# Six sets of products of ones in the early steps, four weight pieces' low halves on TensorE, maxima subtracted on VectorE, and a new order of all steps

## Chip, cores and metric

One core of a Trainium2 chip runs the whole kernel. The metric is device microseconds of one execution, median of several runs.

## What is computed

Attention over four sequences of 768 positions with 8 heads of 64, where each query sees its neighbours nearer than 16 positions and 24 block summaries (maximum of 32 keys, mean of 32 values), followed by a two-layer MLP with gelu on the 3072 tokens:

```python
k_sum = k.reshape(B, H, nb, block, D).max(axis=3)
v_sum = v.reshape(B, H, nb, block, D).mean(axis=3)
mask_l = np.abs(pos[:, None] - pos[None, :]) < window
scores_s = scale * np.einsum('bhsd,bhnd->bhsn', q, k_sum) + np.log(block)
a = np.exp(scores_all - np.max(scores_all, axis=-1, keepdims=True))
a = a / (np.sum(a, axis=-1, keepdims=True) + 1e-09)
x = np.matmul(a, v_all)                       # to tokens x 512
h = x @ w_in                                  # 512 x 2048
g = 0.5 * h * (1.0 + erf(h / sqrt(2)))
return g @ w_out                              # 2048 x 512
```

w_in and w_out come as 64-bit floats, q, k and v as 32-bit ones.

## The kernel before, in words

The attention is cut into 24 units: unit u is 256 queries of 4 heads, two units make the 256 tokens of a chunk, so chunk c needs units 2c and 2c+1. The first six units compute in f32 on TensorE (steps `f_mask`, `f_scores`, `f_sums`, `f_values`), the others with f16 high and low halves. A unit goes: `f_mask` writes the band's mask into the PSUM tile `pss` (there is one such tile for all units), `f_scores` adds 16 small products, `evac` (ScalarE) copies the scores to SBUF, `maximum` (GpSimd, PARTITION_ALL_REDUCE) takes the maximum over the keys, then the maximum is subtracted and the exponential taken; `f_sums` and `f_values` write the PSUM tile `psv` (one for all units); `norm_take`, `norm_cross`, `norm_rec`, `norm_spread`, `norm_mult` divide by the sums; `x_hi` (ScalarE) and `x_lo` (VectorE) split the result.

In the kernel before the maximum of units 0 to 3 is subtracted on TensorE (`m_shift`, a product of a row of -1 with the maximum, into `pss`) and the exponential reads PSUM (`m_exponent`); from unit 4 on VectorE subtracts (`shift`) and `exponent` reads SBUF. Units 6 and 7 too get their mask by `f_mask` and `evac`.

A piece i of w_in (256 of 2048 columns) goes: `fetch_w_in` (1 MiB), three VectorE steps `wi_bits` that make f32 of the 64-bit words, `wi_hi` (ScalarE, high half to f16), `wi_lo` (VectorE, the rest to f16). `wo_bits`, `wo_hi`, `wo_lo` do the same with w_out. `phase1 c i` is 24 products of chunk c with piece i (high by high, high by low, low by high), `gelu`, `g_hi`, `g_lo` follow, and `phase2` is the second layer. Chunks 4 to 11 get their first layer by a Strassen scheme (`sp`), with sums of weights from `wt_add`, `wt_hi`, `wt_lo`.

Keys' maxima come from `prep_k` (VectorE, from the transfer `fetch_k`), `prep_k_end` splits them (a CAST and a subtraction), `k_pack` (ScalarE) builds the f32 keys of a unit, `sum_vt` (TensorE) sums the values of the first sequence's blocks.

The order of all steps is a string of some 1,670 names, ORDER, which is issued as it stands; each engine and the one DMA queue (SyncE's) works its own steps off in that order, and semaphores let a step wait for its inputs and for the room of its output. Three lines of the program that a reader needs:

```python
self.k32 = kp0[:, r0 : r0 + NR, s0 : s0 + CH + TQ].rearrange(...)   # keys of units 0 to 3: the first fetch_k
ps_h = ctx.enter_context(tc.tile_pool(name="ps_h", bufs=N_PSH, space=PSUM))   # three tiles "psh", in turn
nc.gpsimd.partition_all_reduce(out_ap=self.m32, in_ap=self.s32, channels=P, reduce_op=bass_isa.ReduceOp.max)
```

`setup` opens with 16 products of ones (64x512) on TensorE, into a `psh` tile that nothing reads.

Of the kernel before, what the change touches and what calls it, by code (L numbers as in the profile page):

```python
# [77 lines left out]
sum_vt 0, wi_bits 5 0, wt_add 3 1, wt_add 3 2, wi_lo 3, load_v 0, wi_hi 2, wt_hi 3, evac 1, maximum 1, fetch_vt 2,
wi_bits 5 1, wt_lo 3, load_q 2, sum_vt 1, norm_take 0, norm_cross 0, k_pack 2, m_shift 1, m_exponent 1, sum_vt 2,
norm_rec 0, norm_spread 0, wi_bits 6 0, wi_bits 5 2, wi_bits 6 1, wi_lo 2, wi_hi 5, mean_vt, s_load_vs 0, wi_bits 6 2,  # L80
fetch_w_in 4 4, wi_lo 5, f_mask 2, f_scores 2, evac 2, wi_bits 4 0, wi_bits 4 1, maximum 2, load_v 1, s_load_vs 1,
f_values 0, norm_mult 0, x_hi 0, fetch_w_in 0 0, k_pack 3, f_sums 1, norm_take 1, x_lo 0, load_v 2, norm_cross 1,
wi_bits 4 2, m_shift 2, load_q 3, f_values 1, wi_bits 0 0, m_exponent 2, norm_rec 1, norm_spread 1, f_mask 3,
norm_mult 1, wi_bits 0 1, wi_hi 4, f_scores 3, fetch_w_in 1 1, x_hi 1, x_lo 1, wi_bits 0 2, wi_bits 1 0, evac 3,
fetch_v 1 1, f_sums 2, phase1 0 3, wi_hi 0, wi_hi 6, norm_take 2, fetch_w_in 7 3, wi_bits 1 1, load_k 4, wi_lo 6,
load_vs 2, prep_v 1 1, f_values 2, fetch_k 1 3, norm_cross 2, phase1 0 2, k_sums 0 0, norm_rec 2, norm_spread 2,
phase1 0 5, load_v 3, wi_bits 1 2, fetch_k 1 1, gelu 0 3, norm_mult 2, maximum 3, m_shift 3, wi_hi 1, load_v 4,
m_exponent 3, wi_lo 0, prep_k 1 3, phase1 0 6, gelu 0 5, wi_lo 1, wi_bits 7 0, load_vs 3, prep_k 1 1, f_sums 3,
norm_take 3, wi_bits 7 1, fetch_k 1 2, x_hi 2, f_values 3, load_q 4, prep_k 1 2, gelu 0 2, g_hi 0 3, fetch_v 1 2, g_lo
0 3, g_hi 0 2, norm_cross 3, norm_rec 3, g_hi 0 5, phase1 0 0, x_lo 2, k_pack 4, fetch_k 1 0, norm_spread 3, norm_mult  # L90
3, x_hi 3, phase1 0 1, gelu 0 1, fetch_v 1 0, wi_bits 7 2, g_lo 0 5, g_hi 0 1, x_lo 3, load_vs 4, f_mask 4, f_scores
4, wi_hi 7, evac 4, gelu 0 6, prep_k 1 0, maximum 4, wi_lo 7, phase1 1 3, prep_v 1 2, f_mask 5, prep_v 1 0, g_lo 0 2,
g_hi 0 6, gelu 1 3, g_lo 0 1, g_lo 0 6, load_k 5, fetch_w_out 1 5, wo_bits 1 0, k_pack 5, shift 4, fetch_w_out 0 4,
load_k 6, phase1 1 7, g_hi 1 3, wo_bits 1 1, phase1 0 7, gelu 1 7, g_hi 1 7, g_lo 1 7, exponent 4, wo_bits 1 2, gelu 0
7, wo_bits 0 0, wo_bits 0 1, wo_bits 0 2, load_q 5, phase1 1 1, gelu 0 0, g_hi 0 0, f_sums 4, g_hi 0 7, f_values 4,
gelu 1 1, wo_hi 1, g_lo 0 0, norm_take 4, f_scores 5, norm_cross 4, g_lo 0 7, phase1 1 6, g_hi 1 1, evac 5, wo_lo 1,
gelu 1 6, s_k_hi 6, fetch_w_out 3 5, wi_lo 4, norm_rec 4, load_q 7, load_v 6, phase1 1 2, norm_spread 4, norm_mult 4,
fetch_w_out 2 4, g_lo 1 3, phase1 1 4, maximum 5, wo_hi 0, wo_lo 0, f_mask 6, gelu 1 2, phase1 1 5, load_mask, k_lo 6,
fetch_v 1 3, shift 5, load_v 5, exponent 5, prep_k_end 1 0, load_k 8, wo_bits 3 0, g_lo 1 1, wo_bits 3 1, phase1 1 0,
gelu 1 0, g_hi 1 2, prep_v 1 3, wo_bits 3 2, phase2 0 0, g_hi 1 6, k_sums 1 0, load_vs 5, gelu 1 5, g_hi 1 5, f_sums  # L100
5, wo_hi 3, wo_bits 2 0, g_lo 1 2, norm_take 5, wo_bits 2 1, phase1 0 4, s_q_hi 7, x_hi 4, wo_bits 2 2, wo_hi 2, wo_lo
3, load_vs 6, q_lo 7, scores 6, s_k_hi 8, wo_lo 2, prep_k_end 1 1, fetch_w_out 5 5, f_values 5, k_sums 0 1, k_lo 8,
x_lo 4, phase2 0 1, norm_cross 5, evac 6, maximum 6, norm_rec 5, norm_spread 5, norm_mult 5, fetch_w_out 4 4, phase2 0
3, gelu 1 4, wo_bits 5 0, v_hi 6, wo_bits 5 1, f_mask 7, x_hi 5, x_lo 5, g_hi 1 4, g_lo 1 4, gelu 0 4, g_lo 1 5,
phase2 0 2, phase1 2 4, wo_bits 4 0, g_lo 1 6, gelu 2 4, phase1 2 1, wo_bits 4 1, wo_bits 4 2, load_v 8, load_k 7,
s_k_hi 7, phase1 2 0, g_hi 0 4, wo_hi 4, gelu 2 1, load_q 8, wo_bits 5 2, wo_hi 5, shift 6, wo_lo 4, load_vs 8, phase1
2 2, fetch_w_out 7 5, g_hi 1 0, g_lo 0 4, wo_lo 5, s_q_hi 8, gelu 2 0, g_lo 1 0, phase2 0 4, exponent 6, s_p_hi 6,
k_lo 7, phase1 2 6, v_lo 6, fetch_w_out 6 4, k_sums 1 1, scores 7, q_lo 8, v_hi 8, p_lo 6, gelu 2 6, sums 6, wo_bits 7
0, wo_bits 6 0, wo_bits 7 1, load_k 9, wo_bits 6 1, wo_bits 6 2, values 6, s_k_hi 9, evac 7, phase2 0 5, phase1 2 7,
wo_bits 7 2, wo_hi 6, wo_lo 6, wo_hi 7, fetch_k 2 3, load_q 9, g_hi 2 0, load_v 7, load_vs 7, wo_lo 7, k_lo 9, scores  # L110
8, norm_take 6, add_mask 8, phase2 0 6, norm_cross 6, norm_rec 6, norm_spread 6, s_q_hi 9, g_hi 2 1, phase2 0 7, store
0 0, maximum 7, v_lo 8, q_lo 9, shift 7, exponent 7, s_p_hi 7, phase2 1 0, norm_mult 6, load_q 11, s_q_hi 11, phase2 1
2, g_hi 2 4, phase2 1 4, wt_add 4 0, put 0 0, prep_k 2 3, p_lo 7, sums 7, v_hi 7, store 0 1, fetch_v 2 0, v_lo 7,
wt_add 4 1, wt_add 4 2, load_v 9, put 0 1, load_k 11, load_vs 9, g_lo 2 4, g_hi 2 6, norm_take 7, g_lo 2 1, g_lo 2 0,
prep_v 2 0, maximum 8, x_hi 6, phase2 1 6, gelu 2 2, phase1 2 5, norm_cross 7, norm_rec 7, x_lo 6, store 1 0, shift 8,
scores 9, gelu 2 7, q_lo 11, exponent 8, values 7, fetch_v 2 2, wt_hi 4, phase2 1 1, norm_spread 7, wt_lo 4, phase2 1
3, phase2 1 5, add_mask 9, prep_v 2 2, norm_mult 7, load_q 10, phase2 1 7, load_v 11, g_hi 2 2, s_q_hi 10, s_p_hi 8,
s_k_hi 11, load_vs 11, p_lo 8, sums 8, values 8, v_hi 9, v_lo 9, maximum 9, shift 9, fetch_k 2 1, k_lo 11, prep_k 2 1,
g_hi 2 7, g_lo 2 7, scores 11, exponent 9, put 1 0, x_hi 7, phase1 2 3, norm_take 8, load_k 10, x_lo 7, phase1 3 7,
g_lo 2 6, q_lo 10, gelu 2 5, load_v 10, add_mask 11, norm_cross 8, norm_rec 8, fetch_k 2 2, s_p_hi 9, norm_spread 8,  # L120
p_lo 9, s_k_hi 10, phase1 3 5, gelu 2 3, norm_mult 8, store 1 1, gelu 3 5, prep_k 2 2, prep_k_end 2 1, sums 9,
norm_take 9, x_hi 8, phase2 2 1, k_lo 10, scores 10, fetch_k 2 0, put 1 1, values 9, maximum 11, g_hi 2 3, g_lo 2 3,
g_hi 2 5, norm_cross 9, shift 11, exponent 11, wt_add 5 0, s_p_hi 11, load_vs 10, load_k 12, norm_rec 9, norm_spread
9, phase1 3 4, load_q 12, s_q_hi 12, g_lo 2 5, gelu 3 7, v_hi 10, phase1 3 0, gelu 3 4, v_hi 11, g_hi 3 4, norm_mult
9, g_lo 2 2, phase2 2 3, x_hi 9, wt_add 1 0, phase1 3 3, wt_add 1 1, wt_add 1 2, p_lo 11, g_hi 3 5, q_lo 12, wt_hi 1,
add_mask 10, sums 11, gelu 3 3, v_lo 11, g_hi 3 3, prep_k 2 0, phase2 2 5, load_v 12, g_lo 3 4, fetch_v 2 1, phase1 3
6, norm_take 11, wt_add 5 1, norm_cross 11, g_lo 3 3, k_sums 2 1, prep_k_end 2 0, k_sums 2 0, load_q 13, gelu 3 0,
# [111 lines left out]
def band_summary_attention_gelu_mlp(  # L239
# [85 lines left out]
    def setup():
        nc.gpsimd.memset(ones, 1.0)
        if N_FILL:

            fill = ps_h.tile([P, DM], F32, tag="psh", name="psh_fill")
            for _ in range(N_FILL):  # L330
                nc.tensor.matmul(
# [965 lines left out]
```

## Time and profile before

| | us |
|---|---|
| median of 3 runs | 587.44 (587.12 to 587.65) |
| the profiled execution | 588.54 |
| its span, first to last instruction | 586.8 |
| TensorE busy (mean granted clock 0.974) | 568.8 |
| VectorE busy | 459.2 |
| ScalarE busy | 386.5 |
| GpSimd busy | 87.5 |

The span is 1.74 us under the profiled execution's own time, and that time 1.10 us over the median. TensorE is busy 97% of the span; the page's 40 slices show it below 90% in the first three and the last only, and its granted clock below full in the first four. VectorE is busy 8 or 9 tenths up to the middle of the span.

### The profile page before, as it was taken

To read this page: it belongs to the slowest core of one execution; us is meant where nothing else is said; L and a number is where in the kernel's file an instruction comes from. 1 tells how busy PE (TensorE), PEld (TensorE's weight loads), DVE (VectorE), ACT (ScalarE), POOL (GpSimd) and SP (SyncE) were. 2 spreads that over 40 slices of the span, in tenths; PEclk is the share of its full clock that TensorE was granted. 3 is DMA by queue.
4 is the path that set the end of the run, shared out by engine and by line. 5 is a ranking of instruction groups with operands and counts; after the bars stand their busy time and mean duration, and the time that the engine had idled before them with its cause. 6 is when DMAs were issued, how large, how long until landed. Compare 5 with 4: busy or idle time off the path is not lost.

```text
span 586.8 us, 13450 instructions
## 1 busy us (share of the span) xinstructions
PE 568.8 (97%) x5784; PEld 392.8 (67%) x5784; DVE 459.2 (78%) x621; ACT 386.5 (66%) x648; POOL 87.5 (15%) x42
## 2 busy tenths in 40 slices
...
GB/s 290 328 245 279 165 209 292 194 168 131 147 146 167 82 42 159 100 116 121 75 85 75 85 133 4 56 99 79 74 62 1 20 19 19 1 18 2 2 1 91
DMA packets 28652, 64.27 MB, mean 110 GB/s; under 512 B 2736, under 2 KB 7600, under 8 KB 28592
## 3 DMA queue, kind: packets, MB, share of 16 engines
...
## 4 chain that ended last, share of the span: by engine, by line
PE 92%; ACT 2%; POOL 2%; DMA 2%; DVE 2%; issue 1%; POOLq 0%; DVEq 0%; ACTq 0%
PE psy L939 13%; PE pso L987 12%; PE pso L989 11%; PE pso L988 11%; PE psz L939 7%; PE psh L868 5%; PE psh L869 5%; PE psh L870 5%; PE pso_y L1152 4%; PE psx L939 3%; PE pss L649 3%; PE psv L793 3%; PE pss L716 2%; PE pss_x L1152 2%; POOL m L740 2%; DMA q<-in_qd_dram 2%
## 5 line engine op out<-in xcount | busy, mean ns | idle before, releaser
L740 POOL PARTITION_ALL_REDUCE m<-s x24 | 81.3, 3386 | 331.9 <-DVE s L731 113.0
L987 PE MATMUL pso<-w_out_h,gg 128*128 128x512 f16 x320 | 121.5, 380 | 0.0
L988 PE MATMUL pso<-w_out_l,gg 128*128 128x512 f16 x320 | 121.3, 379 | 0.0
L989 PE MATMUL pso<-w_out_h,gg 128*128 128x512 f16 x320 | 121.3, 379 | 0.0
L939 PEld LDWEIGHTS <-wt 128*128 128x128 f16 x768 | 74.5, 98 | 13.6 <-issue 0.8
L868 PE MATMUL psh<-xos,ww 128*128 128x256 f16 x256 | 70.9, 277 | 0.0
L869 PE MATMUL psh<-xos,ww 128*128 128x256 f16 x256 | 70.8, 277 | 0.0
L870 PE MATMUL psh<-xos,ww 128*128 128x256 f16 x256 | 70.8, 276 | 0.0
L939 PE MATMUL psy<-xos,wt 128*128 128x256 f16 x576 | 69.3, 273 | 0.0
L939 PEld LDWEIGHTS <-ww 128*128 128x128 f16 x576 | 55.1, 98 | 11.8 <-issue 0.6
L989 PEld LDWEIGHTS <-gg 128*128 128x128 f16 x320 | 31.3, 98 | 37.8
L987 PEld LDWEIGHTS <-gg 128*128 128x128 f16 x320 | 31.3, 98 | 33.7 <-issue 1.5
L988 PEld LDWEIGHTS <-gg 128*128 128x128 f16 x320 | 31.3, 98 | 31.6
L950 ACT ACTIVATE ww<-psy 128x512 f32<-128x512 f32 x48 | 28.1, 590 | 31.1 <-PE psy L939 30.8
L971 DVE SCALAR_TENSOR_TENSOR gg<-g,gg 128x512 f16<-128x512 f32 x48 | 34.8, 731 | 13.4 <-ACT gg L967 13.4
L957 DVE TENSOR_TENSOR g<-psz,ww 128x512 f32<-128x512 f32 x24 | 16.4, 685 | 20.3 <-PE psz L939 17.6
L967 ACT ACTIVATE gg<-g 128x512 f16<-128x512 f32 x48 | 29.3, 623 | 3.2 <-PE pso L988 2.6
L877 ACT ACTIVATE g<-psh 128x512 f32<-128x512 f32 x32 | 18.8, 594 | 16.8 <-PE psh L870 14.5
L868 PEld LDWEIGHTS <-ww 128*128 128x128 f16 x256 | 25.4, 99 | 6.2 <-issue 2.0
L964 ACT ACTIVATE g<-g 128x512 f32<-128x512 f32 x36 | 22.2, 622 | 8.8 <-DVE g L957 8.8
L869 PEld LDWEIGHTS <-ww 128*128 128x128 f16 x256 | 25.4, 99 | 3.8
L870 PEld LDWEIGHTS <-ww 128*128 128x128 f16 x256 | 25.4, 99 | 3.3
...
## 6 DMA issues: line engine op xcount, KB each, us to landing
...
```

Source lines behind the costliest of these rows:

```text
L740: nc.gpsimd.partition_all_reduce(out_ap=self.m32, in_ap=self.s32, channels=P, reduce_op=bass_isa.ReduceOp.max)
L868: nc.tensor.matmul(ph[:, e, :], wh, xh, start=(k == 0), stop=False)
L869: nc.tensor.matmul(ph[:, e, :], wh, xl, start=False, stop=False)
L870: nc.tensor.matmul(ph[:, e, :], wl, xh, start=False, stop=(k == NCC - 1))
L939: nc.tensor.matmul(ps[:, e, :], ws, xx, start=(first and e == 0 and k == 0 and m == 0), stop=(k == 1 and m == 2), skip_group_check=True,)
L950: nc.scalar.activation(snaps[b, q, n], split8(acc[b, q, "y"]), AF.Copy)
L967: nc.scalar.activation(g_part(o // 2, q, 0, slice(o % 2, 4, 2)), g32t[b, q, o], AF.Copy, scale=SC_G)
L971: nc.vector.scalar_tensor_tensor(out=g_part(o // 2, q, 1, fs), in0=g32t.pop((b, q, o)), scalar=SC_G, in1=g_part(o // 2, q, 0, fs), op0=ALU ...
L987: nc.tensor.matmul(p, gh, w_out_h[:, f, :], start=(f == 0), stop=False)
L988: nc.tensor.matmul(p, gh, w_out_l[:, f, :], start=False, stop=False)
L989: nc.tensor.matmul(p, gl, w_out_h[:, f, :], start=False, stop=(f == NFC - 1))
L1152: nc.tensor.matmul(ps[:, j, :], g, ww_, start=(first and e == 0 and k == 0), stop=(e == 1 and k == 2), skip_group_check=True,)
```

## The change

Three switches turn, a helper for products of ones is made out of `setup`'s loop, and ORDER is another string from its first step to its last:

```diff
-PE_DIFF = 0
-PE_SHIFT = 1
-M16_ROOM = 0
+PE_DIFF = 1
+PE_SHIFT = 0
+M16_ROOM = 1
...
 N_FILL = 16
+N_FILL_STEP = 6
...
-load_q 6, s_q_hi 6, q_lo 6, load_m16, fetch_k 0 0, prep_k 0 0, fetch_w_in 3 3, f_mask 0, load_q 0, prep_k_end 0 0,
-k_pack 0, f_scores 0, fetch_w_in 2 2, wi_bits 3 0, wi_bits 3 1, fetch_k 0 1, wi_bits 3 2, fetch_w_in 5 5, load_q 1,
...
+fetch_k 0 0, prep_k 0 0, k_pack 0, fill 3, prep_k_end 0 0, k_sums 0 0, load_q 0, fill 4, load_m16, fetch_w_in 2 2,
...
+    def products_of_ones(name, n):
+        t = ps_h.tile([P, DM], F32, tag="psh", name=f"psh_fill_{name}")
+        for _ in range(n):
+            nc.tensor.matmul(
+                t[:D].rearrange("p (n d) -> p n d", d=D), ones, ones.unsqueeze(1).broadcast_to([P, DM // D, D]),
+                start=True, stop=True,
+            )
+
+    def fill(k):
+        products_of_ones(k, N_FILL_STEP)
```

Of the steps, these differ in number: `m_shift` and `m_exponent` of units 0 to 3 go, `shift` and `exponent` of these units come (VectorE and ScalarE); `f_mask` and `evac` of units 6 and 7 go, `add_mask` of these units comes (VectorE adds the mask while it reads PSUM); `wi_lo` of pieces 0 to 3 goes, and for each half of these pieces `wi_diff` and `wi_dlo` come; `load_eye` (64 KB), `load_neg` and the six `fill` steps come. Two functions that stood unused before:

```python
def wi_diff(i, h):     # TensorE: 128 * piece - high half, into a psh tile
    nc.tensor.matmul(flat, eye, wt[:, i, h * 512 : (h + 1) * 512], start=True, stop=False)   # f32, 128x512
    nc.tensor.matmul(flat, neg, w_part(i, 0, ks), start=False, stop=True)                    # f16, 128x512
def wi_dlo(i, h):      # ScalarE: to f16
    nc.scalar.activation(w_part(i, 1, ks), flat.rearrange("p (k n) -> p k n", k=2), AF.Copy)
```

With M16_ROOM the small mask lies in the room of `w_out_l`, whose first piece is written after `f_mask 5`.

**TensorE from the scores of unit 0 to the sums of unit 0** (`pss` scores, `kf` keys, `psv` sums and values, `psw` is wi_diff's tile, `eye` and `neg` its constants, `psh_vt` the blocks' sums of v). Before:

```order
L649 MATMUL pss_0_133<-q32_0_138,kf_0_143 128x64 x16
L697 MATMUL pss_0_133<-m32_0_179,neg_1_77 128x512 x2
L620 LDWEIGHTS mask16_sb_78
L620 MATMUL pss_1_192<-mask16_sb_78 128x2x64
...
L649 MATMUL pss_1_192<-q32_1_168,kf_1_188 128x64 x16
L671 MATMUL psv_0_215<-s32_0_177,ones_f_82 32x256 x4
L532 MATMUL psh_vt_220<-w_out_h_87,w_out_l_88 88x512 x4
```

The same place in the change:

```order
L657 MATMUL pss_0_151<-q32_0_139,kf_0_124 128x64 x16
L628 LDWEIGHTS w_out_l_88
L628 MATMUL pss_1_183<-w_out_l_88 128x2x64
...
L426 MATMUL psw_2_0_189<-wt_84,eye_77 128x512
L427 MATMUL psw_2_0_189<-ww_83,neg_78 128x512
L426 MATMUL psw_2_1_212<-wt_84,eye_77 128x512
...
L331 MATMUL psh_fill_5_217<-ones_79 64x512
L331 MATMUL psh_fill_2_226<-ones_79 64x512
L657 MATMUL pss_1_183<-q32_1_192,kf_1_209 128x64 x16
L679 MATMUL psv_0_255<-s32_0_180,ones_f_82 32x256 x4
```

Between the mask of unit 1 and its scores there now stand both halves of piece 2's difference and twelve products of ones (each set is six rows as the one shown); the subtraction of the maximum is gone from TensorE.

**ScalarE at the same place** (L407 and L415 are wi_hi, L727 and L735 evac, L633/L635 and L641/L643 k_pack, L703 m_exponent, L756 exponent, L432 wi_dlo, L526 k_sums, L357 load_neg). Before:

```order
L633 ACTIVATE kf_0_143<-w_out_l_88 128x10x64
L635 ACTIVATE kf_0_143<-ks_f_81 128x2x4x32
L407 ACTIVATE ww_83<-wt_84 128x4x256
L727 ACTIVATE s32_0_177<-pss_0_133 128x1024
L633 ACTIVATE kf_1_188<-w_out_l_88 128x10x64
L635 ACTIVATE kf_1_188<-ks_f_81 128x2x4x32
L703 ACTIVATE s32_0_177<-pss_0_133 128x1024
```

Now:

```order
L641 ACTIVATE kf_0_124<-w_out_l_88 128x10x64
L643 ACTIVATE kf_0_124<-ks_f_81 128x2x4x32
L526 ACTIVATE k_hi0_90<-ks16_0_0_134 128x2x4x24
L526 ACTIVATE k_lo0_92<-ks16_0_0_134 128x2x4x24
L415 ACTIVATE ww_83<-wt_84 128x4x256
L735 ACTIVATE s32_0_180<-pss_0_151 128x1024
L357 ACTIVATE neg_78<-eye_77 128x128
L432 ACTIVATE ww_83<-psw_2_0_189 128x2x256
L641 ACTIVATE kf_1_209<-w_out_l_88 128x10x64
L643 ACTIVATE kf_1_209<-ks_f_81 128x2x4x32
L756 ACTIVATE s32_0_180<-s32_0_180 128x1024
L735 ACTIVATE s32_1_253<-pss_1_183 128x1024
```

In both, the high half of the first piece stands ahead of the copy of unit 0's scores.

**VectorE in the change, from the subtraction of unit 0's maximum to that of unit 1's** (L753 is shift, L380/L385/L389 the three steps of wi_bits, L822 norm_take, L513 prep_k, L521/L522 prep_k_end, L418 wi_lo, L838 norm_rec):

```order
L753 TENSOR_TENSOR s32_0_180<-s32_0_180,m32_0_215 128x1024
L385 SCALAR_TENSOR_TENSOR wt_84<-x32s_85,wt_84 128x1024
L389 SCALAR_TENSOR_TENSOR wt_84<-gg_89,wt_84 128x1024
L389 SCALAR_TENSOR_TENSOR wt_84<-x32s_85,wt_84 128x1024
L822 STREAM_TRANSPOSE dent_0_262<-psv_0_255 128x256
L513 TENSOR_REDUCE ks32_1_194<-kp_1_0_200 128x24
L521 CAST ks16_1_0_265<-ks32_1_194 128x48
L522 TENSOR_TENSOR ks16_1_0_265<-ks32_1_194,ks16_1_0_265 128x48
L418 SCALAR_TENSOR_TENSOR ww_83<-wt_84,ww_83 128x4x256
L838 RECIPROCAL rc_0_275<-rc_0_275 128x16
L753 TENSOR_TENSOR s32_1_253<-s32_1_253,m32_1_295 128x1024
```

The two subtractions are new on VectorE, and the transpose of unit 0's sums (L822) now has a piece of the second sequence's keys behind it.

**The DMA queue's first transfers** are, before: q of unit 6 (256 KB), the small mask (80 KB), the keys of heads 0 to 3 (784 KB), w_in piece 3 (1024 KB), q of unit 0 (256 KB), w_in piece 2; in the change: the keys of heads 0 to 3, q of unit 0, the small mask, w_in piece 2, `eye` (64 KB), a piece of the second sequence's keys (392 KB), w_in piece 0, the keys of heads 4 to 7 (784 KB), w_in piece 5. From ORDER: the first chunk's `phase1` goes 3, 2, 5, 6, 0, 1 before, then `phase1 1 3`, then `f_mask 5`; in the change 0, 5, 4, 2, 1, 7, 3, then `f_mask 5`, then `phase1 1 2`. Before, `norm_take` of a unit stands ahead of its `f_values`; in the change `f_values 2` stands ahead of `norm_take 2`, which therefore waits for it (one tile, `psv`).

## Rows read from the trace of the kernel before

**Rows 1.** Busy time by stretch of the early part: stretch, length, then busy us (and instructions) of PE, PEld, DVE, ACT, POOL, the granted TensorE clock, DMA share, GB/s.
```profile
12.00:23.00 11.00, 5.25 (x35) 3.60 (x34) 10.79 (x13) 4.31 (x6) 3.35 (x1) 0.50 0.94 342
23.00:28.50 5.50, 5.50 (x44) 4.01 (x43) 2.96 (x3) 2.67 (x3) 0.00 (x0) 0.50 0.93 359
28.50:32.00 3.50, 3.50 (x8) 1.18 (x5) 2.09 (x4) 2.27 (x8) 3.22 (x1) 0.50 0.70 179
32.00:37.00 5.00, 5.00 (x15) 1.58 (x13) 5.00 (x5) 1.85 (x2) 0.00 (x0) 0.98 1.04 404
37.00:46.00 9.00, 6.21 (x110) 4.45 (x109) 7.44 (x12) 7.40 (x14) 4.76 (x2) 0.99 0.53 187
46.00:51.60 5.60, 5.56 (x42) 3.80 (x42) 4.15 (x5) 2.47 (x3) 0.00 (x0) 0.50 0.86 285
51.60:56.00 4.40, 4.40 (x25) 3.15 (x22) 3.90 (x5) 4.29 (x11) 0.00 (x0) 0.50 0.91 342
```

**Rows 2.** The timeline of PE: start us, us, engine, line, operation, in square brackets the idle time before and what ended it. L649 f_scores, L620 f_mask, L697 m_shift, L671 f_sums, L663 f_values, L532 sum_vt, L868 the first of phase1's three lines (24 products from 63.98 on are one phase1, the next starts at 66.77 with another step).
```profile
0.94 5.56 PE L331 MATMUL psh_fill<-ones 128*64 128x512 f16 x16 [0.94 <-POOL warm L335]
6.43 0.61 PE L620 MATMUL pss<-mask_sb 128*128 128x128 f16 x4
11.55 3.58 PE L649 MATMUL pss<-q,kf 64*128 64x64 f32 x32 [4.51 <-DMA q<-in_qd_dram]
19.70 2.07 PE L697 MATMUL pss<-m,neg 1*128 1x512 f32 x4 [4.57 <-POOL m L740]
34.97 1.95 PE L532 MATMUL psh_vt<-w_out_h,w_out_l 128*88 128x512 f32 x4
37.28 2.00 PE L649 MATMUL pss<-q,kf 64*128 64x64 f32 x32
43.73 1.13 PE L697 MATMUL pss<-m,neg 1*128 1x512 f32 x4 [1.93 <-POOL m L740]
44.79 1.15 PE L663 MATMUL psv<-s,v 128*64 128x64 f32 x32
63.98 0.28 PE L868 MATMUL psh<-xos,ww 128*128 128x256 f16 x1
66.70 0.64 PE L671 MATMUL psv<-s,ones_f 128*32 128x256 f32 x8
74.29 0.60 PE L620 MATMUL pss<-mask_sb 128*128 128x384 f16 x4
76.75 0.28 PE L868 MATMUL psh<-xos,ww 128*128 128x256 f16 x1
```

**Rows 3.** The products of ones by line, 0 to 4 us and 4.6 to 6.5 us: line, engine, operation, shapes, count, then busy us, mean ns.
```profile
L331 PE MATMUL psh_fill<-ones 128*64 128x512 f16 x8 | 3.6, 634 | 0.9 <-POOL warm L335 0.9
L331 PE MATMUL psh_fill<-ones 128*64 128x512 f16 x8 | 2.1, 417 | 0.0
```

**Rows 4.** The timeline of DVE.
```profile
8.05 1.75 DVE L505 TENSOR_REDUCE ks_f<-w_out_l 128x48 f32<-128x1536 f32 x1 [3.21 <-DMA w_out_l<-in_kp_dram]
10.76 0.69 DVE L372 TENSOR_SCALAR wt<-gg 128x1024 int32<-128x1024 int32 x1 [0.50 <-DMA gg<-in_w_in_dram]
11.49 1.23 DVE L377 SCALAR_TENSOR_TENSOR wt<-gg,wt 128x1024 int32<-128x1024 int32 x1
18.26 1.43 DVE L513 CAST ks<-ks_f 128x48 f16<-128x48 f32 x1
75.33 0.68 DVE L848 TENSOR_TENSOR xos<-x32s,xos 128x512 f16<-128x512 f32 x1
75.94 0.94 DVE L505 TENSOR_REDUCE ks<-kp 128x24 f32<-128x768 f32 x1
76.80 1.21 DVE L410 SCALAR_TENSOR_TENSOR ww<-wt,ww 128x1024 f16<-128x1024 f32 x1
```

**Rows 5.** The timelines of ACT and POOL.
```profile
14.01 1.06 ACT L407 ACTIVATE ww<-wt 128x1024 f16<-128x1024 f32 x1 [3.69 <-DVE wt L381]
15.17 1.03 ACT L727 ACTIVATE s<-pss 128x1024 f32<-128x1024 f32 x1
...
16.29 3.35 POOL L740 PARTITION_ALL_REDUCE m<-s  x1 [14.31 <-ACT s L727]
```

**Rows 6.** Groups by line over the whole span: busy us, mean ns of one. L745 shift, L814, L830, L834 the norm steps, L841 the fourth of them (norm_mult), L513 prep_k_end's cast in the later sequences, L554 prep_v, L886 g_lo, L748 the loads of a table before an exponential.
```profile
L745 DVE TENSOR_TENSOR s<-s,m 128x1024 f32<-128x1024 f32 x20 | 24.3, 1217 | 1.8 <-POOL m L740 1.8
L814 DVE STREAM_TRANSPOSE dent<-psv 128x256 f32<-128x256 f32 x24 | 10.7, 447 | 21.1 <-PE psv L807 9.2 <-PE psv L671 7.8 <-PE psv L793 4.0
L834 DVE STREAM_TRANSPOSE dent<-rc 128x512 f32<-128x512 f32 x24 | 17.0, 708 | 0.6
L830 DVE RECIPROCAL rc<-rc 128x16 f32<-128x16 f32 x24 | 5.9, 245 | 2.8 <-ACT rc L827 2.7
L554 DVE TENSOR_REDUCE vs<-vb 96x32 f32<-96x1024 f32 x12 | 14.4, 1208 | 0.6 <-DMA vb<-in_vb_dram 0.6
L513 DVE CAST ks<-ks 128x48 f16<-128x48 f32 x6 | 1.5, 249 | 0.0
L841 DVE TENSOR_TENSOR x32s<-psv,dent 128x512 f32<-128x512 f32 x24 | 16.5, 686 | 2.7 <-PE psv L793 1.5 <-PE psv L663 0.6
L886 DVE SCALAR_TENSOR_TENSOR gg<-g,gg 128x512 f16<-128x512 f32 x32 | 21.9, 696 | 0.5 <-ACT gg L880 0.4
L748 ACT ACT_TABLE_LOAD x18 | 23.1, 1283 | 0.3
```

More of the change, by code (lines that the diff above doesn't have):

```diff
@@ L78 @@
[L78 to L127, printed above, removed]
```

277 lines of the change are left out of this document (162 added, 115 removed).

## The prediction

> **What bounds the kernel now.** I read the busy times by engine first: TensorE is busy 568.8 of 586.8 us, so time can be won only where it idles or where its clock is half. The slices put both into the first 57 us. The windows of that stretch [rows 1] show where: the granted clock is 0.50 (1.2 of 2.4 GHz) from 12 to 32 us and 0.50 again from 46 to 56, and about 0.98 between. The timeline of TensorE [rows 2] names the holes: 4.51 us ahead of the scores of unit 0 (a transfer of q), 4.57 us ahead of the first subtraction of a maximum (GpSimd's maximum), 1.93 us ahead of the second one, and smaller ones. After phase1 1 3 starts at 76.75 TensorE doesn't idle again before the end of the span, so what follows takes 586.8 - 76.75 = 510.05 us, and the change, which leaves the steps behind this point nearly as they are in kind and number, must be judged by when the same point is reached. VectorE is the second engine to watch: it is busy 10.79 of 11 us from 12 to 23 and 5.00 of 5 from 32 to 37 [rows 1].
>
> **The work that is added and removed.** On TensorE at full clock: two records are one f32 product. The one most like wi_diff's is sum_vt's, whose records take 1.95/4 = .49 us; a subtraction's, with one row, follow each other by .27 (four between 43.73 and 44.79) [rows 2]. I take .43, near the first, so a wi_diff is .86 + .21 for its f16 product (as one of ones, below): 1.07, between .75 and 1.19. Eight of them are 8.6 us. A product of ones took .45 us at half clock and .27 at the later rate [rows 3], between .21 (half of .45 less the change) and .27: a set of six is 1.3 to 1.6 us, six sets 7.7 at 1.28. Gone are four subtractions of 1.13 [rows 2], 4.4, and the masks of units 6 and 7, 2 x .6. TensorE gets about 10.7 us **more** work, nearly all before 50 us. It counts only where TensorE comes last.
>
> VectorE gets four subtractions of 1.22 [rows 6] and loses four wi_lo of 1.21 [rows 4]; even. ScalarE gets eight wi_dlo of 512 elements, between half and all of the 1.03 that a copy of 1024 out of PSUM takes [rows 5] (I take .6, near the half), and four table loads of 1.28 [rows 6], in a stretch where it is idle half the time [rows 1]: nothing.
>
> **When the early stage ends.** I follow the new order by hand, each step starting when its engine and its inputs are there.
>
> *To 16 us.* The keys come first in the queue. Before, DVE took them at 8.05 [rows 4] with 336 KB ahead, which is .8 to 1.1 us at the 300 to 400 GB/s of this stretch [rows 1]; so about 7.0, and their reduction of 1.75 [rows 4] ends near 8.7, ahead of TensorE, which works off 28 products (16 end at 6.5, 12 more to 9.1) and the mask (.61) until 9.7. The scores take 2.0 [rows 2] and end at 11.7, where they started at 11.55 before. w_in piece 2 lands at about 10.7, since the same four sizes stand in front as with piece 3 before (DVE 10.76, [rows 4]). Its three steps end at 13.9, its high half (1.06, [rows 5]) at 15.0, and the copy of unit 0's scores, which stands behind it on ScalarE, at 16.0 (1.03, [rows 5]). The mask of unit 1 needs the PSUM tile that this copy reads. So TensorE idles from 11.7 to 16.1: **a hole of 4.4 us**, no smaller than the first one before, which was followed by half clock.
>
> *16 to 27.* I take half clock from 16 to 22, between the bounds of no fall and of 32. Before, TensorE was 100% busy from 23 to 28.5 with scores, mask and sums and stayed at .50; the rise came at 32, 3.5 us after sum_vt had begun, and stood at .98 from there [rows 1]. Here wi_diff's f32 products, the ones most like sum_vt's, begin at about 17.2 and the products of ones follow, so I put the rise a little over 3.5 us behind that. Mask .6, two wi_diff 2.14, two sets of ones 2.56 are 5.3 us at full clock; 6 us at half do 2.95, the rest ends at 24.35; scores of unit 1 to 26.35, sums of unit 0 (.64, [rows 2]) to 26.95. Were the rise at 20, phase1 1 2 would start 1.0 us earlier, and the median would be 581.5. The Trainium skill, page "TensorE: Matmul & The Clock Gate", section "What's actually happening", says that the default state is throttled and "activity releases the throttle", by which any unbroken work behind the hole brings the early rise; the trace speaks against it, since the unbroken stretch from 23 to 28.5 was not released.
>
> The maximum of unit 0 (3.35, [rows 5]) now ends at 19.4 and nothing of TensorE waits for it. VectorE does: the cast of the keys at 18.5 is held until the maximum ends (1.43 for .25, [rows 4, 6]: the cast ended at 19.69, as the maximum of 16.29 + 3.35 did). Then .25, .7 and the subtraction 1.22: 21.7; three steps of weights (1.22 to 1.23): 25.4. It waits 1.6 us for unit 0's sums. So TensorE is last here by 1.6 us, and the added 2.14 + 2.56 us count, less that much.
>
> *27 to 57.* TensorE has, up to phase1 0 0: sum_vt 5.4, two sets of ones 2.6, wi_diff six times at 1.07 (6.4), scores twice (4.0), f_values twice (2.2), masks twice (1.2), one f_sums (.6): 22.5 us, to 49.5. VectorE, with 20.4 us of instructions and 2.4 of a second cast behind the maximum of unit 1 (27.5 to 30.8), reaches x_lo 1 at 49.8: the two are even, so a hole here costs what it lasts. phase1 0 0 takes 2.7 (66.70 - 63.98, [rows 2]), f_sums 2 .6, phase1 0 5 2.7, f_values 2 1.1: 56.6.
>
> *57 to 76.* norm_take 2 now waits for f_values 2, and VectorE idles about 2.4 us there; behind it stand 24 instructions to x_lo 3: two each of the norm steps L814, L830, L834, L841 (.45, .25, .71, .69), of x_lo (.68), of the first and second weight steps (.69, 1.23), of prep_v (1.21) and prep_k (.94), three third steps (1.22), a subtraction, a wi_lo (1.22, 1.21) and a g_lo (.69) [rows 4, 6]: 20.5 us, less 1.0, since one that is queued starts .04 to .09 before its predecessor's end (75.33 + .68 against 75.94, [rows 4]). x_lo 3 ends at 76.1 and **phase1 1 2 starts at 76.3**. TensorE alone would be there earlier: five phase1 (13.2), three masks and sums (1.8), f_values 3 (1.1), scores 4 (2.0) make 74.7.
>
> *The end.* At that point, against phase1 1 3 at 76.75 before, one phase1 more is done (2.7), the mask of unit 5 (.6; 74.29, [rows 2], is such a one), and two masks never come (1.2). The rest takes 510.05 - 4.5 = 505.6, the span 581.9: 4.9 less than 586.8. Measured as the profiled execution that is 588.54 - 4.9 = 583.6; that execution lies 1.10 over the median of the runs, so the forecast is **582.5 us**. A coarse second sum agrees: of the 30 us at half clock some 24 were work (the rest holes), which goes to 6 and gives 9 us; the holes of the early stage go from 14.5 us to about 7; and 10.7 us of work are added: a gain of about 6 by rounder numbers.
>
> Costs at nothing: the last steps' shares (the mask by VectorE's add for units 6 and 7, M16_ROOM) lie behind 76 us, where VectorE's sums by the same durations stay ahead of TensorE by over 2 us, but for two places, .5 us at phase2 0 5 (wo_lo 5) and 1.0 at phase1 2 4 (x_lo 5).
>
> **The rivals.** One us of half clock from 16 on costs .5 us.
> *No fall.* The clock stays full through the hole of 4.4 us. For: TensorE has run 12 products more ahead of it, without a break. Against: both holes of this length were followed by 0.50 [rows 1, 2]. TensorE gains 3.0 us: span 578.9, median 579.5 (up to 580.5 where VectorE holds it).
> *A longer first stretch.* The half clock lasts to 26 or 32, as it did before until 32 through continuous work. The span is 583.9 (end at 26) to 586.9 (at 32), the median 584.5 to 588.0.
> *A second fall*, the slower side. Before, the clock fell again at 46, after TensorE had been busy 6.21 of 9 us from 37 to 46 with scores, sums, subtractions and holes of .8 and 1.93 [rows 1, 2]. A like mix (f_values, scores, single wi_diff that wait for ScalarE) stands at 37 to 49 now. If a hole there starts a stretch of 6 to 10 us at half clock, that alone costs 3 to 5 us, and the kernel stays faster; added to a first stretch up to 26 or longer it decides: beyond 12 us of half clock over my six the gain is gone. Medians 588.4 to 590.3. The Trainium skill, page "TensorE: Matmul & The Clock Gate", section "HAM oscillation — how this bites in real kernels", describes a clock that falls again at every hole; in the rows it fell at the two clusters of holes and not at each.
> *A wait behind 76.* With .5 us to spare at phase2 0 5, a VectorE that comes 3 to 8 us late there (a slower piece of w_out, a queue with the keys ahead of it) becomes a hole of the same size, and it may fall to half clock: medians 585.5 to 590.5.
> That the change doesn't do what it says is excluded for the order, which stands as told, and open only for the clock.
>
> **How the numbers follow.** About 0.2% (1.2 us) is what a measurement of this kernel can tell from no change: 586.3 to 588.6. Forecast .45, no fall .15, longer stretch .18, second fall .10, wait behind .12. Faster gets all of the first two, .13 of the third and .01 of the fifth: .74. Same gets .05, .02 and .03 of the last three: .10. Slower .16. The range 578.8 to 588.0 takes in the forecast's bounds (wi_diff at 1.19 would add 1.0 us where TensorE is last, sets at 1.6 another 1.3) and all but the upper part of the last two: .83 of the chance.
>
> **What would show it.** In the profile of the changed kernel: a hole of about 4.4 us on TensorE near 11.7, ended by ScalarE's copy; half clock from about 16 to 22 and full from there; the maximum of unit 0 at 16 to 19.4 with a cast of about 1.4 us behind it; phase1's first product near 49.5; phase1 1 2 near 76.3, waiting for x_lo 3; no hole after. A half clock that lasts beyond 26, a second fall between 37 and 50, or a hole after 80 would make the number wrong; phase1 1 2 later than 82 would make the sign wrong.

## The result and the profile after

The change made the kernel slower: 592.41 us median (six runs, 591.29 to 593.09) against 587.28 of the kernel before, ratio 1.0094, 95% interval 1.0069 to 1.012. The forecast was 582.5, with 578.8 to 588.0 as its range.

| profiled execution, us | before | after | difference |
|---|---|---|---|
| span | 586.8 | 589.5 | +2.7 |
| TensorE busy | 568.8 | 574.6 | +5.8 |
| TensorE idle (span less busy) | 18.0 | 14.9 | -3.1 |
| work at half clock, half of it lost | 25.0, 12.5 | 10.1, 5.05 | -7.4 |
| work at full clock (busy less lost) | 556.3 | 569.6 | +13.2 |

Half clock before is 20.5 us less 5.75 us of holes, and 10.2 us (the stretches of [rows 1]); after it is one stretch of 13.7 us, from 64.0 to 77.7, less 3.6 us of hole. The three terms -3.1, -7.4 and +13.2 make the +2.7. Runs of one kernel here differ by up to 5 us with the granted clock (before, spans of 581.3 to 582.2 at a mean clock of 0.982, 585.1 to 586.5 at 0.974; the change, 589.5 at 0.988, 591.1 to 591.3 at 0.985 and 0.986), and the profiled execution of before was among its slower ones and that of the change among its two fastest, so the medians lie 5.1 apart and the two profiled spans 2.7.

By stretch (stretch, length, then busy us and instructions of PE, PEld, DVE, ACT, POOL, granted clock, DMA share, GB/s), which answers to [rows 1]:

```profile
12.00:16.00 4.00, 1.68 (x12) 0.97 (x11) 3.96 (x5) 2.17 (x3) 1.48 (x1) 1.00 1.04 398
16.00:22.00 6.00, 6.00 (x52) 3.54 (x54) 5.93 (x7) 2.61 (x5) 2.23 (x1) 1.00 1.06 406
22.00:50.00 28.00, 28.00 (x236) 15.69 (x229) 26.89 (x32) 22.76 (x39) 8.33 (x3) 1.00 0.92 314
50.00:57.00 7.00, 7.00 (x88) 6.12 (x87) 4.91 (x6) 4.92 (x13) 3.22 (x1) 1.00 1.03 347
57.00:65.00 8.00, 4.39 (x43) 3.19 (x40) 8.00 (x9) 5.00 (x8) 1.03 (x1) 0.94 0.32 102
65.00:76.00 11.00, 8.42 (x78) 7.42 (x79) 7.89 (x10) 7.04 (x16) 3.34 (x2) 0.50 0.33 104
```

Up to 57 us there is full clock (1.00, 2.4 GHz) and, but for one hole at 12 to 16, unbroken work. Then, where DVE is busy 8.00 of 8 us, TensorE does 4.39 of 8, and behind that the clock is at half. TensorE's timeline, which answers to [rows 2], has the places (in square brackets the idle time before, and what ended it; L628 f_mask, L426 wi_diff's f32 product, L657 f_scores, L679 f_sums, L671 f_values, L876 the first of phase1's lines):

```profile
9.62 0.61 PE L628 MATMUL pss<-w_out_l 128*128 128x128 f16 x4
10.16 2.00 PE L657 MATMUL pss<-q,kf 64*128 64x64 f32 x32
14.48 0.60 PE L628 MATMUL pss<-w_out_l 128*128 128x128 f16 x4 [2.32 <-ACT s L735]
14.92 1.02 PE L426 MATMUL psw<-wt,eye 128*128 128x512 f32 x2
17.16 2.78 PE L331 MATMUL psh_fill<-ones 128*64 128x512 f16 x12
21.80 0.64 PE L679 MATMUL psv<-s,ones_f 128*32 128x256 f32 x8
45.19 0.27 PE L876 MATMUL psh<-xos,ww 128*128 128x256 f16 x1
51.20 1.15 PE L671 MATMUL psv<-s,v 128*64 128x64 f32 x32
63.07 0.64 PE L679 MATMUL psv<-s,ones_f 128*32 128x256 f32 x8 [2.32 <-ACT s L756]
67.58 1.98 PE L671 MATMUL psv<-s,v 128*64 128x64 f32 x32 [3.88 <-issue]
81.04 0.27 PE L876 MATMUL psh<-xos,ww 128*128 128x256 f16 x1
```

phase1's first product stands at 45.19, 4.3 us ahead of the forecast; phase1 1 2 starts at 81.04, 4.7 us behind it. Most of the loss stands between these rows: 2.32 us ahead of the sums of unit 3, 3.88 ahead of its values, and then half clock (1.98 for the values where 1.15 is the full rate). What TensorE waits for is VectorE's timeline (L822 norm_take, L389, L385, L380 weight steps, L753 shift, L562 prep_v, L418 wi_lo, L856 x_lo, L513 prep_k):

```profile
52.39 0.45 DVE L822 STREAM_TRANSPOSE dent<-psv 128x256 f32<-128x256 f32 x1 [2.05 <-PE psv L671]
52.77 2.81 DVE L389 SCALAR_TENSOR_TENSOR wt<-gg,wt 128x1024 int32<-128x1024 int32 x1
58.70 2.08 DVE L385 SCALAR_TENSOR_TENSOR wt<-gg,wt 128x1024 int32<-128x1024 int32 x1
60.71 1.21 DVE L753 TENSOR_TENSOR s<-s,m 128x1024 f32<-128x1024 f32 x1
63.05 1.21 DVE L562 TENSOR_REDUCE vs<-vb 96x32 f32<-96x1024 f32 x1
64.17 1.21 DVE L418 SCALAR_TENSOR_TENSOR ww<-wt,ww 128x1024 f16<-128x1024 f32 x1
65.31 0.68 DVE L856 TENSOR_TENSOR xos<-x32s,xos 128x512 f16<-128x512 f32 x1
65.91 1.21 DVE L389 SCALAR_TENSOR_TENSOR wt<-gg,wt 128x1024 int32<-128x1024 int32 x1
67.04 0.44 DVE L822 STREAM_TRANSPOSE dent<-psv 128x256 f32<-128x256 f32 x1
67.41 2.04 DVE L385 SCALAR_TENSOR_TENSOR wst<-xos,wst 128x1024 int32<-128x1024 int32 x1
76.69 0.95 DVE L513 TENSOR_REDUCE ks<-kp 128x24 f32<-128x768 f32 x1 [3.76 <-DMA kp<-in_kp_dram]
77.56 0.68 DVE L856 TENSOR_TENSOR xos<-x32s,xos 128x512 f16<-128x512 f32 x1
```

The subtraction of unit 3 ends at 61.92, its exponential on ScalarE runs 61.96 to 63.02, and the sums start at 63.07:

```profile
61.96 1.06 ACT L756 ACTIVATE s<-s 128x1024 f32<-128x1024 f32 x1 [2.20 <-DVE s L753]
```

The values of unit 3 write the PSUM tile from which norm_take 3 (67.04 to 67.48) reads; they start at 67.58. This profile names no releaser there ("issue"), but the two times agree, and the profile of e10 below puts the same wait down to that transpose (TensorE's timeline):

```profile
68.06 1.98 PE L671 MATMUL psv<-s,v 128*64 128x64 f32 x32 [2.83 <-DVE dent L822]
```

Between sums and values VectorE works on prep_v, wi_lo, x_lo and a weight step, all ahead of norm_take 3 in its order. Three weight steps take 2.81, 2.08 and 2.04 us where 1.21 (the row at 65.91) to 1.23 (L377 in [rows 4]) is their time, each beside a GpSimd instruction:

```profile
52.60 3.22 POOL L748 PARTITION_ALL_REDUCE m<-s  x1 [5.60 <-PE psv L671]
58.67 1.03 POOL L608 COPY v<-w_out_h 24x1024 f32<-24x1024 f32 x1 [2.85 <-DMA v<-in_vw_dram]
66.58 1.80 POOL L608 COPY v<-w_out_h 24x1024 f32<-24x1024 f32 x1 [6.87 <-DMA v<-in_vw_dram]
```

Behind 81 us four more holes stand, at 165.6, 262.3, 363.9 and 473.1 us, .54 to .69 us each, 2.35 in all, where before had none. Two are again values that wait for a norm_take, two wait for a copy on ScalarE.

### The profile page after: what moved, and what is told of

Read it like the earlier page. It is cut to its first block, busy times and chain, and to the rows that moved or that the text cites. A ratio compares the mean times of both kernels' runs of the same rounds, so it can differ in the third digit from the quotient of the medians.

```text
span 589.5 us, 13534 instructions
## 1 busy us (share of the span) xinstructions
PE 574.6 (97%) x5820; PEld 395.3 (67%) x5820; DVE 457.3 (78%) x623; ACT 393.8 (67%) x659; POOL 90.3 (15%) x41
## 4 chain that ended last, share of the span: by engine, by line
PE 92%; ACT 2%; DVE 2%; issue 1%; DMA 1%; SPq 0%; ACTq 0%
PE psy L947 14%; PE pso L995 12%; PE pso L997 11%; PE pso L996 11%; PE psz L947 7%; PE psh L876 5%; PE psh L878 4%; PE psh L877 4%; PE pso_y L1160 4%; PE psx L947 3%; PE psv L801 3%; PE pss L724 2%; PE pss L657 2%; PE pss_x L1160 2%; PE psw L426 1%
## 5 line engine op out<-in xcount | busy, mean ns | idle before, releaser
L748 POOL PARTITION_ALL_REDUCE m<-s x24 | 83.6, 3483 | 349.7 <-DVE s L739 97.0
L947 PEld LDWEIGHTS <-wt 128*128 128x128 f16 x768 | 74.1, 98 | 13.5 <-issue 0.6
L876 PE MATMUL psh<-xos,ww 128*128 128x256 f16 x256 | 71.0, 277 | 0.0
L947 PEld LDWEIGHTS <-ww 128*128 128x128 f16 x576 | 55.4, 98 | 11.9 <-ACT ww L958 1.8
L979 DVE SCALAR_TENSOR_TENSOR gg<-g,gg 128x512 f16<-128x512 f32 x48 | 32.8, 697 | 10.4 <-ACT gg L975 10.4
L753 DVE TENSOR_TENSOR s<-s,m 128x1024 f32<-128x1024 f32 x24 | 29.0, 1210 | 2.1 <-POOL m L748 2.1
L756 ACT ACTIVATE s<-s 128x1024 f32<-128x1024 f32 x24 | 25.4, 1057 | 7.7 <-DVE s L753 7.4
L972 ACT ACTIVATE g<-g 128x512 f32<-128x512 f32 x36 | 22.3, 625 | 11.1 <-DVE g L965 10.9
L876 PEld LDWEIGHTS <-ww 128*128 128x128 f16 x256 | 25.4, 99 | 5.3 <-issue 0.7
L965 DVE TENSOR_TENSOR g<-psz,ww 128x512 f32<-128x512 f32 x24 | 16.5, 686 | 15.9 <-PE psz L947 12.5
```

The lines of the kernel that those rows point to most:

```text
L753: nc.vector.tensor_tensor(out=self.s32, in0=self.s32, in1=self.m32, op=ALU.subtract)
L876: nc.tensor.matmul(ph[:, e, :], wh, xh, start=(k == 0), stop=False)
L947: nc.tensor.matmul(ps[:, e, :], ws, xx, start=(first and e == 0 and k == 0 and m == 0), stop=(k == 1 and m == 2), skip_group_check=True,)
L979: nc.vector.scalar_tensor_tensor(out=g_part(o // 2, q, 1, fs), in0=g32t.pop((b, q, o)), scalar=SC_G, in1=g_part(o // 2, q, 0, fs), op0=ALU ...
```

## The experiments

**Undo the lateness of unit 3.** e1 moves two VectorE steps of the change forward (`shift 3`, `norm_take 3`) and two behind them (`g_lo 0 0`, `prep_v 1 2`):

```diff
-maximum 3, norm_mult 2, ... g_hi 0 4, shift 3, g_hi 0 0, wo_bits 0 0, g_lo 0 0, prep_v 1 2, fetch_k 2 1, exponent 3, f_sums 3, wi_lo 7,
-... wi_bits 6 2, k_pack 4, norm_take 3, gelu 0 2,
+maximum 3, shift 3, norm_mult 2, ... g_hi 0 4, g_hi 0 0, wo_bits 0 0, fetch_k 2 1, exponent 3, f_sums 3, norm_take 3, g_lo 0 0, prep_v 1 2,
+wi_lo 7, ... wi_bits 6 2, k_pack 4, gelu 0 2,
```

> The change with two VectorE steps of unit 3 moved ahead of others on their engine: shift 3 directly behind maximum 3, norm_take 3 directly behind f_sums 3 (g_lo 0 0 and prep_v 1 2 go behind it). Theory A (the loss lies where TensorE waits for unit 3's exponential and transpose, holes of 2.3 and 3.9 us, and in the half clock of 13.7 us behind them): both holes shrink to under 1 us each, the clock stays full from 60 to 80, phase1 1 2 starts at 74 to 76 in place of 81.1, median 584 to 587. Rival B (TensorE's added work, 12 us at full clock, is the loss, wherever the holes are): VectorE stays as late, other holes take their place, median 591 to 593.5 as the change.

586.63 us (12 runs, 584.65 to 589.32), ratio to before 1.0017 (0.9995 to 1.0039): 5.8 us under the change by the medians, 4.5 by the ratios to before (1.0094 less 1.0017). The hole ahead of the sums is gone, that ahead of the values is 1.44, and one of 1.18 ahead of the scores of unit 4 appears (k_pack 4 waits for prep_v 1 2, which the edit had moved back). In the profile the clock is at half from about 16.3 to 19.7 us, behind the first of these rows, and from 67.3 to 74.1, behind the other two (TensorE's timeline):

```profile
14.87 0.60 PE L628 MATMUL pss<-w_out_l 128*128 128x128 f16 x4 [2.80 <-ACT s L735]
64.99 1.15 PE L671 MATMUL psv<-s,v 128*64 128x64 f32 x32 [1.44 <-POOL v L608]
67.32 3.68 PE L657 MATMUL pss<-q,kf 64*128 64x64 f32 x32 [1.18 <-ACT kf L643]
```

A few steps of VectorE in another place, with all the added work left in, give back the loss: the interval takes in no change to before. Theory A holds for the time. It had three things wrong: "under 1 us each", the full clock from 60 to 80 in this profile, and phase1 1 2, which starts at 78.18 and not at 74 to 76.

**Keep the clock up in the holes.** e2 puts products of ones into them:

```diff
-... exponent 3, f_sums 3, ... f_values 3,
+... exponent 3, fill 6, fill 7, f_sums 3, ... fill 8, fill 9, f_values 3,
```

> The change with twelve more products of ones ahead of f_sums 3 and twelve ahead of f_values 3, 5.4 us of work into the two holes of 6.2 us; no other step is moved. Theory A: TensorE waits for VectorE there, so the work costs nothing, and the clock, which fell at 63.8 and came back at 77.5, stays full; the work of 65 to 77 gets about 5 us shorter: median 587 to 589. Rival B (work counts): 5.4 us more, 597 to 598. Rival C (the clock falls without the holes or costs nothing there): 592 to 593.

588.82 us, ratio 1.0031 (1.0014 to 1.0048): 3.6 us under the change, with 5.4 us more work. The two stretches that were at 0.94 and 0.50 are at full clock (columns as above):

```profile
57.00:65.00 8.00, 7.94 (x58) 4.76 (x56) 8.00 (x10) 5.57 (x8) 1.03 (x1) 1.00 0.40 136
65.00:76.00 11.00, 9.92 (x121) 8.45 (x120) 8.91 (x12) 6.64 (x14) 5.08 (x2) 1.00 0.45 139
```

Work put where TensorE waits for VectorE cost little: the values of unit 3 start .67 us behind the end of norm_take 3, in place of .10. By this and the 3.6 us the half clock had cost some 4 us by itself, an estimate. It goes with the holes: e1 and e2 remove most of the same loss by different means.

**Take work away while VectorE is last.** e3 drops `fill 5`, `fill 2`, `fill 1` and `fill 0` from the change's order.

> The change without the four sets of ones that stand after the first hole (two ahead of the scores of unit 1, two ahead of wi_diff 0 0): 5.4 us less work on TensorE between 16 and 31 us. Theory A (VectorE sets the time from 12 to 78; it was busy there almost without a break): no gain, and larger holes with more half clock are possible, 591 to 596. Rival B (work counts): 586 to 588.

590.64 us, ratio 1.0064 (1.0044 to 1.0084), 1.8 us under the change (the intervals overlap) for 5.4 us less work. New holes of 1.29, .49 and .40 us at 18 to 32, half clock from 19.8 to 26.6, and the holes at unit 3 still 1.86 and 3.88: two thirds of the saving went there. Between the two theories, nearer to A.

**Undo the part with the low halves.** e6:

```diff
-wi_diff i 0, ... wi_dlo i 0, ... wi_diff i 1, ... wi_dlo i 1,
+... wi_lo i, ...            (at the place of wi_dlo i 0, pieces 0 to 3)
```

> The change with the low halves of the w_in pieces 0 to 3 back on VectorE (wi_lo where wi_dlo stood; no wi_diff, no wi_dlo), the rest as it is. TensorE loses 9.5 us of work, ScalarE 4.8, VectorE gets 4.8 more. Theory A (VectorE sets the stretch from 12 to 78 us): the work saved turns into holes and half clock, 590 to 595. Rival B (work on TensorE counts in full): 583 to 585.

597.85 us, ratio 1.0188 (1.0167 to 1.021), 5.4 us **over** the change although TensorE has 9.5 us less to do. VectorE is busy 23.48 of 24 us, TensorE 17.12 (same columns):

```profile
12.00:26.00 14.00, 9.27 (x60) 4.74 (x60) 13.64 (x13) 5.29 (x7) 5.22 (x2) 0.88 1.04 398
26.00:50.00 24.00, 17.12 (x161) 10.83 (x159) 23.48 (x27) 14.17 (x26) 5.23 (x2) 0.78 0.69 243
```

This is the strongest sign for A: with 4.8 us more on VectorE the kernel takes 5.4 more, and 9.5 us less on TensorE bought nothing. It was beyond the range that A gave; in the profile the clock is at half for 30.7 us, 13.7 in the change. In this order the part with wi_diff is a gain. The other part that moves work between the two engines, the subtraction on VectorE, was undone in no run of this order, so what it costs here stays open.

**Single parts in the order of the kernel before.** e7 puts `shift` and `exponent` where `m_shift` and `m_exponent` of units 0 to 3 stood; e5 adds `fill 0`, `fill 1` behind `f_mask 0` and `fill 2`, `fill 3` ahead of `m_shift 0`; e11 puts `wi_diff i 0, wi_dlo i 0, wi_diff i 1, wi_dlo i 1` where `wi_lo i` stood, with `load_eye`, `load_neg` and M16_ROOM.

> The kernel before with one part of the change alone: the maximum of units 0 to 3 is subtracted on VectorE (shift and exponent at the places of m_shift and m_exponent). TensorE loses 4.2 us of work and the two waits for a maximum (4.57 and 1.93 us) and the one for the exponential (1.18); VectorE, busy 10.79 of 11 us there, gets 4.9 more. Theory A (VectorE sets): 586 to 591. Rival B (TensorE sets): 577 to 581.

> The kernel before with 12 products of ones in each of its two large holes (ahead of the scores of unit 0, and ahead of the first subtraction of a maximum), nothing else changed. If the full clock of the changed kernel's first 60 us comes from unbroken products before and in the hole, the half clock from 12 to 32 us goes here too. Theory A (VectorE sets the early stage of this kernel as well, busy 10.79 of 11 us from 12 to 23): gain of 0 to 3 us, 584.5 to 587.5. Rival (TensorE's clock sets it): some 14 us of work at half clock become 7, median 579 to 582.

> The kernel before with one part of the change alone: the low halves of w_in pieces 0 to 3 by TensorE and ScalarE (wi_diff and wi_dlo at the places of wi_lo, with load_eye, load_neg and M16_ROOM). TensorE gets 9.5 us of work, ScalarE 4.8, VectorE loses 4.8. Theory A (VectorE sets the early stage, so that each us taken from it is worth up to one, and TensorE's work partly fits into holes): 582 to 588. Rival B (TensorE's work counts): 592 to 597.

e7: 589.65, ratio 1.0055 (1.0033 to 1.0077). The waits for the maxima are gone from TensorE, as is 4.2 us of its work, but the sums of unit 1 now wait 4.76 us for VectorE (norm_mult 0), and the kernel is 1.9 to 4.5 us slower: A.

```profile
42.71 1.08 PE L679 MATMUL psv<-s,ones_f 128*32 128x256 f32 x8 [4.76 <-DVE x32s L849]
```

e5: 586.34, ratio 0.9995 (0.9977 to 1.0013), no change. The mean clock rose to 0.980 to 0.988 from 0.974 to 0.982 and 5.4 us of work were added, mostly into the two holes (the first is gone in its profile, the second is 3.44 in place of 4.57). That is in the range of theory A; why the better clock gained nothing was not tried further. e11: 611.24, ratio 1.0414 (1.0389 to 1.0438), which neither theory had. The edit stood in a bad place: on TensorE wi_diff 3 comes behind sum_vt 0, at 32.24, and ScalarE, whose next step was wi_dlo 3, waited 10.9 us for it with the copy of unit 1's scores and the high halves queued behind, and VectorE 13.76 us for those. It says nothing on the part itself in that order, which stays open.

**What GpSimd does to VectorE.** e10 makes ScalarE do one GpSimd copy of the change (`load_vs 3` becomes `s_load_vs 3`).

> The change with one copy moved from GpSimd to ScalarE: the block means of unit 3's values (load_vs 3, GpSimd 58.67 to 59.70 in the change). In the change the weight step on VectorE that started at 58.70 beside it took 2.08 us in place of 1.23. If GpSimd's access holds VectorE, that step takes 1.2 us here, shift 3 and the sums of unit 3 come .85 us earlier, and the median falls by about 1 us: 591 to 592. If the 2.08 us has another cause, it stays, and so does the time, 592 to 593.

591.18, ratio 1.0073 (1.0052 to 1.0094), 1.2 us under the change, in the range expected, but the intervals overlap. The sums of unit 3 did not come earlier: counted from norm_take 2 they start 10.79 us behind it (10.68 in the change), since the copy on ScalarE pushed the exponential's table load back. The values do, by .9 us (14.27 behind in place of 15.19). The rows (VectorE, then GpSimd):

```profile
60.10 1.21 DVE L385 SCALAR_TENSOR_TENSOR wt<-gg,wt 128x1024 int32<-128x1024 int32 x1
67.93 1.18 DVE L385 SCALAR_TENSOR_TENSOR wst<-xos,wst 128x1024 int32<-128x1024 int32 x1
```

```profile
66.89 3.12 POOL L608 COPY v<-w_out_h 24x1024 f32<-24x1024 f32 x1 [9.67 <-DMA v<-in_vw_dram]
```

Without the copy beside it the first step takes 1.21 in place of 2.08. The second met the other copy in a different order: the copy started while VectorE was in a weight step, and now the copy took 3.12 (1.80 in the change) and the weight step 1.18 (2.04). So either engine can hold the other up. The Trainium skill, page "SBUF — State Buffer", section "SBUF: two separate sides", calls the port pair that the two share an exclusive lock, which the one that starts first gets for its whole instruction. The first step (2.08 beside the copy, 1.21 without) agrees; the weight step at 67.93, which starts 1.04 us behind the copy and is not held, is not explained by it.

**All waits closed.** e8 is e1 with prep_v 1 2 left ahead of norm_take 3 and wo_bits 0 0 put behind it, and three more moves; e9 drops `fill 5`, `fill 2`, `fill 1`, `fill 0` from it, e12 `fill 3` and `fill 4` too:

```diff
-... wi_hi 2, f_scores 0, evac 0, ... fetch_v 1 0, ... f_values 2, ... norm_take 2, fetch_v 1 2, load_v 3,
+... f_scores 0, evac 0, wi_hi 2, ... load_v 3, fetch_v 1 0, ... norm_take 2, f_values 2, ... fetch_v 1 2,
```

> The change with the waits of its first 70 us closed by order alone: shift 3 behind maximum 3, norm_take 3 behind f_sums 3 (wo_bits 0 0 and g_lo 0 0 behind it, prep_v 1 2 stays ahead), norm_take 2 ahead of f_values 2, load_v 3 ahead of fetch_v 1 0 on the queue, evac 0 ahead of wi_hi 2. Theory A: e1 (586.6) had holes of 2.80, 1.44 and 1.18 us and 2.0 us of idle VectorE ahead of norm_take 2; without them 581 to 584. Rival: each closed wait opens the next on VectorE, 585.5 to 587.

> As e8_waits_closed, and without the four sets of products of ones behind the first hole (5.4 us of TensorE's work). If TensorE's work is what is left, 5 us under e8; if VectorE sets the time, within 1.5 us of e8, with holes in their place and the clock lower.

> As e9_waits_closed_no_ones, and without the two sets of ones ahead of the first mask as well, so that none of the six is left. If these two sets keep the clock up through the wait for the first weights, it is at half for longer behind 12 us and the time is 1 to 3 us over e9 (586 to 588). If they are only work, up to 2.7 us under e9 (582 to 584.5).

e8 585.96, ratio to before 0.9991 (0.9972 to 1.0009); e9 584.75, 0.9973 (0.9958 to 0.9989); **e12 583.29, 0.9946 (0.993 to 0.9963)**, the fastest of all and under both kernels. The hole ahead of unit 3's sums is gone in all three and the one ahead of its values is .62. What is late next is unit 3's result: ScalarE's x_hi 3 and then x_lo 3, the wait that the forecast had named (TensorE's timeline of e8; the second row is the seventh product of phase1 1 2, the first that reads unit 3):

```profile
63.09 1.15 PE L671 MATMUL psv<-s,v 128*64 128x64 f32 x32 [0.62 <-issue]
74.31 0.27 PE L876 MATMUL psh<-xos,ww 128*128 128x256 f16 x1 [1.70 <-ACT xos L853]
75.10 0.27 PE L877 MATMUL psh<-xos,ww 128*128 128x256 f16 x1 [0.53 <-DVE xos L856]
```

phase1 1 2 itself starts at 71.79 there, at 69.98 in e9 and 71.20 in e12 (81.04 in the change, 76.3 told), and its seventh product at 74.31, 72.60 and 72.97. e8 gained only .7 over e1, less than hoped. e9 gained 1.2 over e8 for 5.4 us of work: VectorE still sets part of the stretch (A), but no longer all. e12 went against the first expectation: without the two early sets the scores of unit 0 and the mask of unit 1 come earlier (the mask at 11.04 in place of 12.67 in e9), and the clock is little worse (in the profile at half for two stretches of 3.4 and 6.8 us; a mean of 0.989 over the twelve runs, 0.992 in e9). So in this order, once unit 3 doesn't wait, the six sets together cost 2.7 us (e12 against e8; the intervals don't overlap); each single step from e8 to e9 to e12 is within them.

## Why the prediction was wrong

Right: the mask and the scores of unit 0 (9.6 and 10.2 to 12.2; told 9.1, 9.7 and 11.7), the hole behind them, ended by ScalarE's copy; the work from the sums of unit 0 to phase1 0 0 (22.44 to 45.19, 22.75 us; told 22.5); phase1 0 0 to f_values 2 (7.1 each); norm_take 2 behind f_values 2 with 2.05 us of idle VectorE (told 2.4); no second fall between 37 and 50; the maxima off TensorE's path.

Better than told: the first keys were there at 5.12 (told 7.0), which TensorE could not use yet; the hole was 2.32 us, not 4.4, since piece 2 had landed at 9.21 (told 10.7, "since the same four sizes stand in front"), and behind it the clock stayed full in this run (the rival *No fall*, to which .15 was given). Together that put phase1 0 0 4.3 us ahead. These gains hide a part of what was lost later.

**The step that failed** is *57 to 76*, in its last sentence: "TensorE alone would be there earlier", with f_sums 3 and f_values 3 in the sum as work of .6 and 1.1. VectorE was priced by when its last row, x_lo 3, ends. But TensorE needs two rows out of the middle of that chain, shift 3 (through the exponential) and norm_take 3, and behind norm_take 3's late place the values, scores 4 and two phase1 were queued. TensorE lost 6.2 us there and got no phase1 done meanwhile, and when it reached phase1 1 2 at 81.04, x_lo 3 had been ready since 78.24: the row that the prediction took for the last was not. e1 shows that this one place is worth the whole loss against before. The half clock behind it (5.05 us of loss; e2 gives back 3.6 for all its added work) wasn't in any rival, since all of them put a fall before 50 or a hole behind 76.

That is not the whole miss of 9.9 us. Of it 4.7 us is phase1 1 2 (81.04 for 76.3); 2.9 us lies behind it, where the rest took 508.5 us (told 505.6), 2.35 of them the four small holes, in a stretch whose costs the prediction had put at nothing; and 2.3 us is the median over the profiled span, 2.9 us here and .6 in the forecast. By the prediction's own sum 81.04 meant a span of 586.6, no change, so its sign to watch, "later than 82", missed the second of these terms. The four holes stand in all the variants of the change above; no run removes them.

Sizes in the sums were off as well. VectorE's chain from norm_take 2 to x_lo 3 took 25.9 us (52.39 to 78.24), told 19.5: 3.3 us of holds by GpSimd (2.81 + 2.08 + 2.04 less 3.67), which I had priced for casts ahead of 31 us only, though the trace of before had them at this place too (the rows below, where 1.21 is the time), and 3.76 us for a transfer of keys that the queue could issue only when the scores of unit 4, themselves late, had ended. The added work was 12.3 us and not 10.7: eight wi_diff take 9.5 (starts 1.07 to 1.27 apart, the upper half of my .75 to 1.19 and over it), six sets 8.1, less 4.2 and 1.1.

```profile
58.54 2.31 DVE L410 SCALAR_TENSOR_TENSOR ww<-wt,ww 128x1024 f16<-128x1024 f32 x1
61.64 1.64 DVE L410 SCALAR_TENSOR_TENSOR ww<-wt,ww 128x1024 f16<-128x1024 f32 x1
```

And the coarse second sum shows what the detail hid: told, clock -9, holes -7.5, work +10.7; measured, -7.4, -3.1, +13.2. The first two terms were taken as if the whole early stage would run by TensorE, while the rows of VectorE (10.79 of 11 us in [rows 1]), which the prediction itself names, said that it would not. *A wait behind 76* was the nearest rival; it looked behind 76 us, and the two holes stood at 60.8 to 67.6.
